# Attention plus gMLP block: the second chunk's modulation issued two pieces behind a product over two blocks instead of four over one, and the last spatial weight sums put behind other products

## The chip, the cores and the metric

The kernel runs on one core of a Trainium2 chip. The metric is device time in microseconds (us), median of several executions. PE is TensorE, PEld its weight loads, DVE is VectorE, ACT is ScalarE.

## The reference, cut to what matters

```python
def _B_ref(x, w_in, w_sp, b_sp, w_out):      # S = 2048, D = 1024, Fh = 1792
    z = _gelu(jnp.einsum('bsd,df->bsf', x, w_in))
    z1 = z[..., :Fh].copy()
    z2 = _layernorm(z[..., Fh:], axis=-1)
    g = jnp.einsum('ts,bsf->btf', w_sp, z2) + b_sp[None, :, None]
    return jnp.einsum('bsf,fd->bsd', z1 * g, w_out)
# ... attention comes first (32 heads), then:
h = _layernorm(x, axis=-1) * (1 + cb) + sb   # the "modulation" of this study
x = x + gb * _B_ref(h, B_w_in, B_w_sp, B_b_sp, B_w_out)
```

Attention fills the time up to about 1130 us, its output projection the time up to 1320 us. The change touches the products of `h` with `w_in` (1310 to 1490 us), and the preparation of `w_sp` for the spatial product that follows.

## The kernel before

Each matrix product is done in blocks of two by two. Seven sub-products take the place of eight, at the price of sums of operands (on VectorE, ahead of TensorE) and of results (ScalarE copies a PSUM bank out, a "snap"; VectorE adds another bank to it). A `Block` has seven products, numbered 1 to 7; bank "a" serves 1, 6, 5 and 3 in turn, so TensorE can't start product 6 before ScalarE has copied what 1 left. `hooks` are functions queued right after a given product; this is where all side work is placed.

```python
BANK = {1: "a", 6: "a", 5: "a", 3: "a", 2: "c", 7: "b", 4: "b"}
def finish(self, n):
    ps = self.ps[self.BANK[n]]
    if n == 1:   self.s = self.snap(ps, 1)                      # ScalarE copy
    elif n == 2: self.out(1, 1, ps, self.s)                     # VectorE sum, gelu two products later
    elif n == 6: self.x = self.snap(ps, 2)
    elif n == 5: self.out(2, 2, self.ps["b"], self.snap(ps, 3))
    elif n == 3: self.out(1, 2, ps, None)
    elif n == 4: self.out(2, 1, ps, self.x)
    for fn in self.hooks.get(n, ()):
        fn()
    # ... functions put off by after(n, fn) run here when their count is down
```

Two streams of blocks are interleaved product by product (`dual`). Each stream runs product 1 of a block, then 3 and 4 of its previous block, then 2, 6, 7, 5. The second chunk (rows 1024 to 2047) is modulated in place once its transposed load has landed, sixteen pieces of 128x512 in four quarters:

```python
def mod_h(c, i, j):
    t = hT[c, i, j]
    for dc in range(4):
        k = 8 + 4 * j + dc
        if c == 0:
            nc.scalar.activation(t[:, dc, :], t[:, dc, :], ACT.Identity,
                                 scale=cols_l[:, 8 + k:9 + k], bias=cols_l[:, k:k + 1])
        else:
            nc.vector.tensor_scalar(out=t[:, dc, :], in0=t[:, dc, :], scalar1=cols_l[:, 8 + k:9 + k],
                                    scalar2=cols_l[:, k:k + 1], op0=ALU.mult, op1=ALU.add)
# ...
for n, m in enumerate((3, 1, 2, 4)):
    # ... loads of the quarters
    z2b[3].on((1, 2, 6, 7)[n], lambda q=HQ[(n + 2) % 4]: mod_h(1, *q))   # four pieces at once
    z1b[2].on((1, 2, 6, 7)[n], lambda m=n + 1: h_sum(1, m))              # needs the modulated quarters
```

Near the end of the stage, the hooks of z1 block n make the four small weight sums of z1 block n+1 (`w1_sum`, after products 2, 6, 7 and 5). Behind them, at the same four hooks, one task each is taken from a list; the last eight tasks are the last sums over `w_sp` (128x1024):

```python
b.on((2, 6, 7, 5)[k - 1], lambda m=m, k=k: w1_sum(*seq[m], k))
# ...
z2b[15].on(4, ..., lambda: tasks.extend(sums[8:]), ...)
for b in z2b[9:] + z1b[7:]:
    for m in (2, 6, 7, 5):
        b.on(m, work())
```

In the profiles these are: L1217 the modulation on VectorE, L1214 the modulation on ScalarE, L1388 a small weight sum, L1440 a spatial sum, L1043 the sum of a bank and a snap, L1038 a snap, L1320 a gelu, L1465 a piece of layer norm on VectorE, L995 every product of these blocks.

The softmax here doesn't subtract the row's maximum and nothing guards it: scores larger than these inputs give would overflow.

Of the kernel before, what the change touches and what calls it, by code (L numbers as in the profile page):

```python
# [16 lines left out]
def kernel(  # L17
# [1111 lines left out]
    for n in range(2, 6):  # L1129
        for k, m in enumerate((6, 7, 7, 5)):  # L1130
            q = 4 * (n - 2) + k
# [69 lines left out]
    def load_h(c, i, j):  # L1201

        t = hT[c, i, j] = heap.take("hT", [P, 4, 512], FP16)
        t0 = c * 1024 + i * 512
        nc.sync.dma_start(out=t[:], in_=h2_dram[t0:t0 + 512, j * 512:(j + 1) * 512],
                          transpose=True)

    def mod_h(c, i, j):

        t = hT[c, i, j]  # L1210
        for dc in range(4):
            k = 8 + 4 * j + dc
            if c == 0:
                nc.scalar.activation(t[:, dc, :], t[:, dc, :], ACT.Identity,  # L1214
                                     scale=cols_l[:, 8 + k:9 + k], bias=cols_l[:, k:k + 1])
            else:
                nc.vector.tensor_scalar(out=t[:, dc, :], in0=t[:, dc, :],  # L1217
                                        scalar1=cols_l[:, 8 + k:9 + k],
                                        scalar2=cols_l[:, k:k + 1], op0=ALU.mult, op1=ALU.add)

    def h_sum(c, n):

        s = hs.setdefault(c, {})
        s[n] = hT[c, 1, 0] if n == 3 else heap.take(f"hs{n}", [P, 4, 512], FP16)
        a, b = {1: (hT[c, 1, 0], hT[c, 1, 1]), 2: (s.get(1), hT[c, 0, 0]),
                3: (hT[c, 0, 0], hT[c, 1, 0]), 4: (hT[c, 0, 1], s.get(2))}[n]
        fn = nc.vector.tensor_add if n == 1 else nc.vector.tensor_sub
        fn(out=s[n][:], in0=a[:], in1=b[:])
# [15 lines left out]
    def w2_sum(k, n):  # L1244

        t = w2t.setdefault(k, {})
        t[n] = w2[k, 0, 1] if n == 1 else heap.take(f"w2_t{n}", [P, 4, FC], FP16)
        a, b = {1: (bf(w2[k, 0, 1][:]), bf(w2[k, 0, 0][:])), 2: (bf(w2[k, 1, 1][:]), t.get(1)),
                3: (bf(w2[k, 1, 1][:]), bf(w2[k, 0, 1][:])),
                4: (bf(w2[k, 1, 0][:]), t.get(2))}[n]  # L1250
        nc.vector.tensor_sub(out=t[n][:], in0=a[:], in1=b[:])
# [34 lines left out]
    HQ = ((1, 0), (1, 1), (0, 0), (0, 1))  # L1286
    for n, q in enumerate(HQ):
        (wos[5] if n < 3 else wos[6]).on((6, 7, 5, 1)[n], lambda q=q: load_h(0, *q))
        wos[6].on((2, 6, 7, 5)[n], lambda q=q: mod_h(0, *q))
# [47 lines left out]
    def z2_block(c, k, m):  # L1337
        def operands(n):
            h = h_op(c, n)
            b = {1: (0, 0), 2: (1, 0), 3: (1, 1)}.get(n)  # L1340
            w = bf(w2[(k,) + b][:]) if b else w2t[k][{4: 4, 5: 1, 6: 2, 7: 3}[n]][:]
            return ([h[:, dc, m * P:(m + 1) * P] for dc in range(4)],
                    [w[:, dc, :] for dc in range(4)])

        def out(i, j, ps, snap):
            ti = 8 * c + 4 * (i - 1) + m
            f0 = (j - 1) * 2 * FC + k * FC
            z = short("z2")[:, 0:FC]
            gelu(z, ps, snap)

            def stats():
                nc.vector.bn_stats(out=z_st[:, ti, 2 * (j - 1) + k, :], in_=z)
                nc.sync.dma_start(z2_dram[ti, :, f0:f0 + FC], z)
                left_[ti] -= 1
                if not left_[ti]:
                    nc.vector.bn_aggr(out=z_mv[:, ti, :], in_=z_st[:, ti])
            after(4, stats)

        b = Block(operands, copy_snap, out, FC)
        b.on(4, lambda: done_with_h(c))  # L1360
        return b
# [28 lines left out]
    def z1_block(c, p):  # L1390
        def operands(n):
            h = h_op(c, n)
            b = {1: (0, 0), 2: (1, 0), 3: (1, 1)}.get(n)
            if b:
                w = [w1[c, p][:, 4 * b[0] + dc, b[1] * P:(b[1] + 1) * P] for dc in range(4)]
            else:
                w = [w1t[c, p][:, {4: 3, 5: 0, 6: 1, 7: 2}[n], dc, :] for dc in range(4)]
            return w, [h[:, dc, :] for dc in range(4)]

        def out(i, j, ps, snap):  # L1400
            if (c, p) not in z1T:
                z1T[c, p] = heap.take("z1T", [P, 2, 1024], FP16)
            gelu(z1T[c, p][:, j - 1, (i - 1) * 512:i * 512], ps, snap)

        b = Block(operands, copy_snap, out)
        b.on(4, lambda: done_with_h(c))
        return b
# [7 lines left out]
    def load_w(c, k, j):  # L1415

        t0 = c * 1024 + j * 512
        for u in range(2):
            t = W[k, j, u] = heap.take(f"w{k}{j}", [P, 4, 512], FP16)
            nc.sync.dma_start(out=bf(t[:]), in_=B_w_sp[t0:t0 + 512, (2 * k + u) * 512:  # L1420
                                                       (2 * k + u + 1) * 512], transpose=True)
# [67 lines left out]
    def work(n=1):  # L1489
        def go():  # L1490
            for _ in range(n):
                if tasks:
                    tasks.pop(0)()
        return go

    seq = [(c, p) for c in range(2) for p in range(NG)]
    z2b = [z2_block(c, k, m) for k in range(2) for c in range(2) for m in range(4)]
    z1b = [z1_block(*s) for s in seq]
# [5 lines left out]
    for n, s in enumerate(seq):  # L1504
        b = z1b[n]
# [8 lines left out]
    z2b[2].on(7, lambda: load_w2(1))  # L1514
    for n, m in enumerate((3, 1, 2, 4)):
        (wos[7] if n < 2 else z2b[0]).on((3, 4, 7, 5)[n], lambda q=HQ[(n + 2) % 4]: load_h(1, *q))
        z2b[3].on((1, 2, 6, 7)[n], lambda q=HQ[(n + 2) % 4]: mod_h(1, *q))
        z1b[2].on((1, 2, 6, 7)[n], lambda m=n + 1: h_sum(1, m))
        z2b[4 + n // 2].on((7, 5)[n % 2], lambda m=m: w2_sum(1, m))
        z2b[6 + n].on(2, lambda n=n: load_w(0, *WQ[n]))  # L1520
# [3 lines left out]
        z2_norms(), [load_z(0, p, k) for p in range(2) for k in range(2)])))  # L1524
    z2b[9].on(1, lambda: tasks.extend(scale_w() + sums[:8]))
    for b in z2b[9:] + z1b[7:]:
        for m in (2, 6, 7, 5):
            b.on(m, work())
    z1b[9].on(4, lambda: load_b(0))
    norms = []  # L1530
# [326 lines left out]
```

## Time and profile before

| | before |
|---|---|
| median of the first 3 runs | 1757.61 us (1756.5 to 1757.78) |
| span of the profiled run (its time: 1754.26 us) | 1752.4 us |
| PE busy | 1734.1 us, 99% |

The page's first lines and the first line of its chain of waits:

```profile
span 1752.4 us, 23647 instructions
...
PE 1734.1 (99%) x8414; PEld 795.6 (45%) x8414; DVE 1522.7 (87%) x2324; ACT 1297.7 (74%) x1530; POOL 31.3 (2%) x39
...
PE 93%; DVE 4%; DMA 1%; ACT 1%; issue 1%; SPq 0%; DVEq 0%; ACTq 0%
```

TensorE is the bound, so only a moment in which it stands still can be won. Busy time is the wrong place to look for those (a matmul's record outlasts the distance to the next one: 379 ns against 216 ns), so the useful reading is the distance between starts. Four matmuls of 512 columns that are not held up take 0.86 us, four of 448 columns 0.76 us. The timeline of TensorE (start, duration, engine, line, operation, out<-in, count, idle before it) then shows the stops around the modulation:

```profile
1351.48 1.03 PE L995 MATMUL a<-hT,w_13040 128*128 128x512 f16 x4
1352.71 0.92 PE L995 MATMUL b<-s_slots,h_slots 128*128 128x448 f16 x4 [0.20 <-DVE sum L1043]
1354.29 1.02 PE L995 MATMUL a<-tx,h_slots 128*128 128x512 f16 x4 [0.66 <-ACT snap L1038]
```

From 1351.48 to 1352.71 is 1.23 us where 0.86 would do, a gap of 0.37; from 1352.71 to 1354.29 is 1.58 where 0.76 would do, a gap of 0.83. The bracket alone understates both, since it counts from a modelled end. What kept the sum and the snap is in the timelines of VectorE and ScalarE:

```profile
1349.57 1.36 DVE L1217 TENSOR_SCALAR hT<-hT,cols_l 128x512 f16<-128x512 f16 x4
...
1352.04 0.61 DVE L1043 TENSOR_TENSOR sum<-b,snap 128x448 f32<-128x448 f32 x1
```

```profile
1352.69 0.58 ACT L1320 ACTIVATE z_13178<-sum 128x448 f16<-128x448 f32 x1 [2.67 <-DVE sum L1043]
1353.17 1.07 ACT L1038 ACTIVATE snap<-a 128x512 f32<-128x512 f32 x2
```

VectorE has no idle time from 1348 to 1355 (in the table of windows below, 7.00 of 7), and the lump of four at 1349.57 belongs to a product that ended near 1346.6, so it is some 3 us behind. The sum of bank "b" runs at 1352.04, and TensorE waits for that bank. A gelu on ScalarE waits 2.67 us for the same sum, and the snap that frees bank "a" stands behind the gelu. So one late sum stops TensorE twice. A third gap of 0.29 us follows at 1363.1.

The second place is at 1471 to 1475 us, first TensorE, then VectorE:

```profile
1470.80 1.03 PE L995 MATMUL b<-hT,w_t 128*128 128x512 f16 x4
1471.80 1.04 PE L995 MATMUL a<-hs_13248,s_slots 128*128 128x512 f16 x4
1472.68 1.03 PE L995 MATMUL a<-hs_13196,w_t 128*128 128x512 f16 x4
1474.27 1.04 PE L995 MATMUL b<-hT,s_slots 128*128 128x512 f16 x4 [0.57 <-DVE s_slots L1388]
```

```profile
1471.66 0.68 DVE L1440 TENSOR_TENSOR h_slots<-w_13586,h_slots 128x1024 f16<-128x1024 f16 x1
...
1473.19 0.68 DVE L1440 TENSOR_TENSOR w_t_14467<-w_13588,w_13499 128x1024 f16<-128x1024 f16 x1
1473.79 0.42 DVE L1388 TENSOR_TENSOR s_slots<-h_slots 128x512 f16<-128x512 bf16 x1
```

The weight sum that TensorE wants at 1473.5 is only begun at 1473.79, behind two spatial sums (L1440) that nobody wants before 1490. The gaps are 0.14 and 0.73 us.

The busy times of this table of windows are quoted later (columns: stretch, its length, then busy time and instructions per engine):

```profile
1334.00:1348.00 14.00, 14.00 (x72) 6.85 (x71) 12.52 (x30) 8.75 (x17) 0.00 (x0) 1.00 1.00 296
1348.00:1355.00 7.00, 6.13 (x30) 2.74 (x29) 7.00 (x17) 3.53 (x7) 0.00 (x0) 1.00 0.33 100
```

### The profile page before, as it was taken

The numbers are of one execution on the slowest core, as the hardware profiler recorded it, in microseconds if no ns is written. First come the engines' busy times: TensorE is split into PE (matmuls) and PEld (weight loads), VectorE is DVE, ScalarE is ACT, GpSimd is POOL, SyncE is SP. The second block draws the span as 40 slices with busy tenths as digits, with TensorE's granted clock in tenths as the row PEclk, the third lists the DMA queues.
The fourth block names the chain that finished last, engine by engine and source line by source line (L and its number), as shares of the span: only waits on it lengthen the run. The fifth ranks groups of instructions, "written<-read, shape, count | busy, mean of one in ns | idle before, by whom it ended". The sixth has DMA issues, their size and how long they took to land.

```text
span 1752.4 us, 23647 instructions
## 1 busy us (share of the span) xinstructions
PE 1734.1 (99%) x8414; PEld 795.6 (45%) x8414; DVE 1522.7 (87%) x2324; ACT 1297.7 (74%) x1530; POOL 31.3 (2%) x39
## 2 busy tenths in 40 slices
PE   7999999999999999999999999999999999999999
PEld 4444444444444444444444444444444444444444
DVE  6898898898988899998999988898889788778975
ACT  6998889999999999999999999711235666737500
POOL 1000000000000000000000000000000000000000
PEclk9999999999999999999999999999999999999999
DMA  8575456645434643544643464758858544548222
GB/s 253 132 183 142 115 142 160 163 121 133 122 95 137 171 104 96 151 141 131 163 120 103 119 186 130 195 138 210 209 159 217 146 120 122 180 120 229 60 78 97
DMA packets 465896, 253.79 MB, mean 145 GB/s; under 512 B 310640, under 2 KB 425584, under 8 KB 465776
## 3 DMA queue, kind: packets, MB, share of 16 engines
q1 hardware_dynamic: 465776, 252.26, 53.9%
q8 instruction: 66, 1.08, 0.3%
q14 instruction: 54, 0.44, 0.1%
HBM read 142.08 MB, written 55.59 MB: 113 GB/s over the span
## 4 chain that ended last, share of the span: by engine, by line
PE 93%; DVE 4%; DMA 1%; ACT 1%; issue 1%; SPq 0%; DVEq 0%; ACTq 0%
PE sps L510 24%; PE ops L787 24%; PE a L995 17%; PE b L995 9%; PE c L995 4%; PE qa L491 4%; PE qps L408 4%; PE qb L491 3%; PE bo L1619 1%; ACT pt L850 1%; DMA wm<-in_w_mod_dram 1%; PE a_11083 L995 1%; DVE sum L1043 0%; DVE stats L155 0%; PE a L1717 0%
## 5 line engine op out<-in xcount | busy, mean ns | idle before, releaser
L850 ACT ACTIVATE pt<-sps 128x1024 bf16<-128x1024 f32 x1008 | 1003.7, 1023 | 77.7 <-PE sps L510 34.8
L510 PE MATMUL sps<-qT,kT 128*128 128x512 bf16 x2048 | 609.2, 379 | 2.3 <-ACT pt L850 1.2
L787 PE MATMUL ops<-pt,v_sb 128*128 128x512 bf16 x2048 | 598.9, 379 | 0.0
L510 PEld LDWEIGHTS <-kT 128*128 128x128 bf16 x2048 | 199.6, 98 | 247.2 <-issue 14.5
L787 PEld LDWEIGHTS <-v_sb 128*128 128x128 bf16 x2048 | 200.1, 98 | 243.2 <-issue 1.6
L1038 ACT ACTIVATE snap<-a 128x512 f32<-128x512 f32 (+1 forms) x111 | 60.5, 564 | 99.2 <-PE a L995 82.8
L995 PEld LDWEIGHTS <-h_slots 128*128 128x128 f16 (+1 forms) x756 | 73.9, 98 | 87.5 <-issue 1.4
L866 DVE COPY ou<-ops 128x512 f32<-128x512 f32 x126 | 81.1, 685 | 31.5 <-PE ops L787 28.8
L408 PE MATMUL qps<-h1T,wq_t 128*128 128x512 bf16 x288 | 96.7, 379 | 0.0
L1468 ACT ACTIVATE zr<-zr,z_nm,z_rs 128x256 f16<-128x256 f16 x96 | 47.9, 586 | 48.2 <-DMA zr<-z_dram 48.2
L1043 DVE TENSOR_TENSOR sum<-b,snap 128x512 f32<-128x512 f32 (+1 forms) x76 | 50.0, 659 | 36.0 <-ACT snap L1038 18.7
L666 DVE TENSOR_TENSOR oT<-ou,rbc 128x1024 bf16<-128x1024 f32 x62 | 75.3, 1215 | 1.1 <-DMA rbc<-rec_dram 1.1
L476 DVE COPY tx<-qa 128x512 f32<-128x512 f32 x66 | 45.4, 688 | 30.6 <-PE qa L491 30.6
L644 DVE TENSOR_REDUCE den<-pT 128x8 f32<-128x1024 bf16 x58 | 68.6, 1183 | 0.0
L491 PE MATMUL qa<-h1s,wq_t 128*128 128x512 f16 x176 | 63.1, 379 | 0.0
L995 PEld LDWEIGHTS <-wq_t 128*128 128x128 f16 (+1 forms) x390 | 38.1, 98 | 45.1 <-issue 0.3
L995 PEld LDWEIGHTS <-s_slots 128*128 128x128 f16 (+1 forms) x363 | 35.4, 98 | 43.3 <-DVE s_slots L1388 1.5
L491 PEld LDWEIGHTS <-wq_t 128*128 128x128 bf16 (+1 forms) x352 | 34.4, 98 | 41.5
L149 POOL TENSOR_TENSOR rstd<-var,neg_half 128x1 f32<-128x1 f32 x30 | 25.9, 862 | 1295.7 <-DVE var L147 1228.4
L471 DVE TENSOR_TENSOR qT<-qb,tx 128x512 bf16<-128x512 f32 x66 | 45.2, 684 | 0.7
L408 PEld LDWEIGHTS <-wq_t 128*128 128x128 bf16 x288 | 28.2, 98 | 33.9 <-issue 0.6
L491 PEld LDWEIGHTS <-tx 128*128 128x128 f16 x264 | 25.8, 98 | 31.2
(979 smaller groups left out, 2576.9 us busy)
## 6 DMA issues: line engine op xcount, KB each, us to landing
rbc<-rec_dram SPq DMA_DIRECT2D x63, 512.0 KB
v_sb<-in_A_v_cache_dram SPq DMA_DIRECT2D x40, 512.0 KB
oT_dram<-oT SPq DMA_DIRECT2D x62, 256.0 KB
sums_dram<-pacc SPq DMA_DIRECT2D x58, 256.0 KB
wm<-in_w_mod_dram SPq DMA_DIRECT2D x8, 1024.0 KB
wq_t<-in_A_wq_dram SPq DMA_DIRECT2D x7, 1024.0 KB
zr<-z_dram SPq DMA_DIRECT2D x12, 512.0 KB
oq<-oT_dram SPq DMA_DIRECT2D x11, 512.0 KB
```

The lines of the kernel that those rows point to most:

```text
L408: nc.tensor.matmul(box["ps"][:], weights[:, dc, hc:hc + DH], src[:, dc, q0:q0 + 512], start=(n == 0), stop=(n == KD - 1))
L491: nc.tensor.matmul(box["b" if m in (2, 7, 4) else "a"][:], *operand(m, dc), start=(m in (1, 2, 7) and dc == 0), stop=(dc == 3), skip_group ...
L510: nc.tensor.matmul(sps[:, j * 512:(j + 1) * 512], kts[h][:, kb * P:(kb + 1) * P], qts[(h, qh)][:, j * 512:(j + 1) * 512], start=True, stop ...
L644: nc.vector.tensor_reduce(out=den[:], in_=state[i]["pT"][:], op=ALU.add, axis=mybir.AxisListType.X)
L666: nc.vector.tensor_mul(out=oT, in0=state[i]["ou"][:], in1=state[i]["rbc"][:])
L787: nc.tensor.matmul(o_ps[j][:], vs[halves[i][0]][:, kb, :], pt_tiles[g][:, j * 512:(j + 1) * 512], start=(kb == 0), stop=(kb == NKB - 1))
L850: nc.scalar.activation(pt_tiles[g], s_tiles.pop(g)[:], ACT.Exp, scale=SCALE, **bias)
L866: nc.vector.tensor_copy(out=ou[:, j * 512:(j + 1) * 512], in_=o_ps[j][:])
L995: nc.tensor.matmul(self.ps[self.BANK[n]], a, b, start=(n in (1, 2, 7) and k == 0), stop=(k == len(lhs) - 1), skip_group_check=True)
L1038: nc.scalar.activation(t, ps, ACT.Copy)
L1043: nc.vector.tensor_add(out=t, in0=ps, in1=snap)
L1468: nc.scalar.activation(z, z, ACT.Identity, scale=z_rs[:, q:q + 1], bias=z_nm[:, q:q + 1])
```

## The change

The intent, by the title that the change came with, is to spread the modulation thinly, two pieces behind a product instead of four, over the third and fourth z2 blocks instead of the fourth alone, one piece on ScalarE and one on VectorE; and to move the last spatial sums away from the hooks where the weight sums are due. The whole diff:

```diff
-    def mod_h(c, i, j):
+    def mod_h(c, i, j, dcs=range(4), by_act=True):
 
         t = hT[c, i, j]
-        for dc in range(4):
+        for dc in dcs:
             k = 8 + 4 * j + dc
-            if c == 0:
+            if by_act:
                 nc.scalar.activation(t[:, dc, :], t[:, dc, :], ACT.Identity,
                                      scale=cols_l[:, 8 + k:9 + k], bias=cols_l[:, k:k + 1])
             else:
@@
-        z2b[3].on((1, 2, 6, 7)[n], lambda q=HQ[(n + 2) % 4]: mod_h(1, *q))
+        for k in range(2):
+            z2b[2 + n // 2].on(((2, 6), (7, 5), (1, 2), (6, 7))[n][k], *[
+                lambda q=HQ[(n + 2) % 4], dc=2 * k + a: mod_h(1, *q, (dc,), not a)
+                for a in range(2)])
@@
     for b in z2b[9:] + z1b[7:]:
-        for m in (2, 6, 7, 5):
+        for m in (2, 6, 7, 5) if b not in z1b[10:] else (1, 3, 7):
             b.on(m, work())
```

## The prediction

> **What bounds the kernel.** TensorE. The engine table gives PE 1734.1 us busy of 1752.4 (99%), at full clock; the chain of waits is 93% PE. The Trainium skill ("Perfetto Trace Analysis", Identifying the Most-Contended Engine) warns that matmul busy time is a poor measure because matmuls are pipelined, so I took distances between matmul starts: 216 ns for 512 columns, 189 ns for 448, back to back almost everywhere. The excess over that is 11.2 us in the first 40 us, 8.0 us through attention, and only 3.1 us between 1300 and 1500 us, which the diff touches. No matmul is added or removed, so the reachable gain lies inside those 3 us.
>
> **Part A: modulation.** Before, sixteen VectorE pieces (128x512 f16; the timeline shows 1.37 us for four) run in lumps at 1339.7, 1344.1, 1345.9 and 1349.6 us. VectorE is 12.5 us busy of 14 in 1334 to 1348 and 7.0 of 7 in 1348 to 1355 (table of windows), and 3 us behind: the last lump belongs to a product that ends near 1346.6. A gelu on ScalarE then waits 2.7 us for a late VectorE sum, the PSUM copy behind it is late, and TensorE stops: 0.37 us at 1352.7 (for a sum), 0.83 at 1354.3 and 0.29 at 1363.1 (for copies). Gaps of 0.32 and 0.44 us at 1327 and 1330.5 lie ahead of this and stay.
>
> After, eight pieces stay on VectorE (0.34 us each; 2.7 us removed) and eight go to ScalarE (2.92 us for four in the first chunk's modulation, 0.73 each, 5.8 us added), one of each per hook, from about 1334.6 to 1347 us. The transposed loads landed at 1324.1, 1328.8, 1334.7 and 1336.7 us, before each quarter's first use, so nothing waits for a load. VectorE's backlog at 1352 should go, and with it 1.2 to 1.5 us of gaps. Against that, ScalarE's 8.75 us busy in 1334 to 1348 become 14.6 of 14: slightly overfull. TensorE needs a copy two to five products (0.76 to 0.87 us each) later; I allow 0 to 0.6 us of new gaps at 1340 to 1349.
>
> **Part B: last spatial sums.** Eight VectorE sums (128x1024, 0.6 us each) run at 1469.3 to 1479.8 us among the small weight sums of the next z1 block, due two products later. TensorE loses 0.14 us at 1471.8 and 0.73 at 1474.3 to those weight sums. After, the eight sit behind products 1, 3 and 7 (on 7 the weight sum precedes them), spread over 1472 to 1488. This recovers 0.5 to 0.87 us. VectorE has little idle in 1476 to 1492 (15.25 of 16 busy), so norm pieces and first gate sums may come 0.6 us later against some 3 us of slack: cost 0 to 0.3 us.
>
> **Sum.** A gains 1.3 less 0.3, B 0.7 less 0.1: about 1.6 us, from 1757.6 to 1756.0 us (0.1%); 8 times in 10 between 1754.4 and 1757.7. Chances: faster by over 2% 0.005, within 2% 0.99, slower by over 2% 0.005.
>
> **What would show it.** No TensorE gap at 1352 to 1355, nor at 1471 to 1475; the last modulation ends before 1348 instead of 1351; ScalarE full near 1334 to 1348; VectorE 2.7 us less busy; span near 1750.8.
>
> **What would make it wrong.** ScalarE's overfull stretch delays copies and stops TensorE near 1340 to 1350 by as much as at 1354; or the later sums hold up norms or gate sums, opening a gap at 1485 to 1496; or the gap at 1354 came from the weight sums beside the modulation and stays.

## The result, and the profile after

Ratios in this document are the mean time of one kernel's runs over that of the other's of the same rounds, so not quite the ratio of the medians quoted.

| | before | after |
|---|---|---|
| median | 1757.05 us (4 runs, 1754.78 to 1757.78) | 1753.49 us (4 runs, 1753.12 to 1754.07) |
| ratio | | 0.9982, 95% interval 0.9965 to 0.9999 |
| span of the profiled run | 1752.4 us | 1752.3 us |

The median lies below the forecast's range, and the two profiled spans are equal although the medians differ by 3.6 us. Both need an explanation. The first lines of the page of after:

```profile
span 1752.3 us, 23530 instructions
...
PE 1728.6 (99%) x8299; PEld 795.6 (45%) x8414; DVE 1522.5 (87%) x2324; ACT 1298.5 (74%) x1530; POOL 30.7 (2%) x39
```

PE's busy time fell by 5.5 us for no good reason: 115 of 8414 matmul records are missing from this trace. All 8414 weight loads are there, in the same order in both, so from here on the traces are laid side by side by weight load. The table gives how much later (positive) or earlier (negative) a given load starts than in the profiled run of before, in us:

| weight load no. (its start in before) | 300 (33 us) | 6300 (1304 us) | 7000 (1447 us) | 7170 (1483 us) | last (1749 us) |
|---|---|---|---|---|---|
| after | +1.09 | +2.19 | +0.71 | -0.18 | +0.10 |

The code up to load 6300 is the same. The changed kernel's profiled run lost 1.09 us in its first 33 us and 1.10 more in attention, before any of the change was reached; it then won 1.48 us at the modulation and 0.89 us at the spatial sums, and gave back 0.28 us, a net 2.09 us. The equal spans are an accident of the start and of attention.

TensorE's timeline where before stopped at 1352.71 and 1354.29:

```profile
1353.66 1.03 PE L995 MATMUL a<-hT,w_13044 128*128 128x512 f16 x4
1354.53 0.92 PE L995 MATMUL b<-s_slots,h_slots 128*128 128x448 f16 x4
1355.28 1.03 PE L995 MATMUL a<-tx,h_slots 128*128 128x512 f16 x4
```

The starts are 0.87 and 0.75 us apart: no gap. VectorE (and ScalarE below) at the same place:

```profile
1350.62 0.72 DVE L1217 TENSOR_SCALAR hT<-hT,cols_l 128x512 f16<-128x512 f16 x2
...
1352.45 0.61 DVE L1043 TENSOR_TENSOR sum<-b,snap 128x448 f32<-128x448 f32 x1
```

```profile
1353.10 0.58 ACT L1320 ACTIVATE z_13178<-sum 128x448 f16<-128x448 f32 x1 [2.02 <-DVE sum L1043]
1353.58 1.07 ACT L1038 ACTIVATE snap<-a 128x512 f32<-128x512 f32 x2
```

This run is 2.18 us late at this point, so the sum at 1352.45 stands at 1350.27 on the clock of before, where it stood at 1352.04: 1.77 us earlier. The snap came forward by the same 1.77 us (1353.58 less 2.18 against 1353.17). VectorE is not less busy; it did the same work sooner, as the windows moved by the same 2 us show:

```profile
1336.00:1350.00 14.00, 14.00 (x72) 6.86 (x71) 14.00 (x35) 9.13 (x18) 0.00 (x0) 1.00 1.01 296
1350.00:1357.00 7.00, 7.00 (x35) 3.27 (x34) 7.00 (x16) 4.56 (x10) 0.00 (x0) 1.00 0.44 127
```

VectorE was idle 1.48 us of the first window before, and is idle no time after. ScalarE has 9.13 us in it, not the 14.6 that the prediction added up: no ScalarE piece was made. The instructions of the ScalarE line confirm it (count, durations in ns, first and last start); the last one starts at 1293 us, and these are the first chunk's:

```profile
L1214 ACT ACTIVATE h_slots<-h_slots,cols_l x8: 801/803/805, 1272.0 to 1282.6; 128x512 f16<-128x512 f16 x8
L1214 ACT ACTIVATE hT<-hT,cols_l x8: 798/801/804, 1284.8 to 1293.0; 128x512 f16<-128x512 f16 x8
```

The second place is clean too (timelines of TensorE and VectorE of after), with the wanted weight sum now begun at 1472.70 (1.8 us earlier, after taking off the 0.71 us by which this run is late):

```profile
1472.37 1.03 PE L995 MATMUL a<-hs_13248,s_slots 128*128 128x512 f16 x4
1473.23 1.03 PE L995 MATMUL a<-hs_13196,w_t 128*128 128x512 f16 x4
1474.10 1.03 PE L995 MATMUL b<-hT,s_slots 128*128 128x512 f16 x4
```

```profile
1472.70 0.42 DVE L1388 TENSOR_TENSOR s_slots<-h_slots 128x512 f16<-128x512 bf16 x1
1473.03 0.69 DVE L1440 TENSOR_TENSOR h_slots<-w_13586,h_slots 128x1024 f16<-128x1024 f16 x1
```

A small stop is new, at 1484 to 1487 us (TensorE's timeline of after). From 1485.36 to 1486.45 is 1.09 us where 0.86 would do:

```profile
1485.36 1.03 PE L995 MATMUL a<-hs_13196,w_t 128*128 128x512 f16 x4
1486.45 1.04 PE L995 MATMUL b<-hT,w_t 128*128 128x512 f16 x4
```

TensorE waits there for weight sums again (L1388, at 1484.02 and 1485.98), which now stand behind moved spatial sums and pieces of the layer norm.

### The profile page after: what moved, and what is told of

Same layout as the page of the kernel before. It is cut to its first block, busy times and chain, and to the rows that moved or that the text cites. A ratio compares the mean times of both kernels' runs of the same rounds, so it can differ in the third digit from the quotient of the medians. Undisturbed runs are those within 1.5% of the kernel's fastest.

```text
span 1752.3 us, 23530 instructions
## 1 busy us (share of the span) xinstructions
PE 1728.6 (99%) x8299; PEld 795.6 (45%) x8414; DVE 1522.5 (87%) x2324; ACT 1298.5 (74%) x1530; POOL 30.7 (2%) x39
## 4 chain that ended last, share of the span: by engine, by line
PE 90%; DVE 5%; DMA 2%; issue 1%; ACT 1%; SPq 0%; DVEq 0%; ACTq 0%
PE ops L787 23%; PE sps L510 22%; PE a L995 17%; PE b L995 9%; PE c L995 5%; PE qa L491 4%; PE qps L408 3%; PE qb L491 3%; PE bo L1622 1%; ACT pt L850 1%; DMA wm<-in_w_mod_dram 1%; PE a_11083 L995 1%; DVE sums_3250 L872 0%; DVE den L644 0%; DVE ou L866 0%
## 5 line engine op out<-in xcount | busy, mean ns | idle before, releaser
L510 PE MATMUL sps<-qT,kT 128*128 128x512 bf16 x1986 | 596.4, 379 | 4.0 <-ACT pt L850 2.1
L995 PEld LDWEIGHTS <-h_slots 128*128 128x128 f16 (+1 forms) x700 | 68.5, 98 | 79.7 <-DVE h_slots L1065 0.3
```

The costliest lines, as they stand in the source:

```text
L510: nc.tensor.matmul(sps[:, j * 512:(j + 1) * 512], kts[h][:, kb * P:(kb + 1) * P], qts[(h, qh)][:, j * 512:(j + 1) * 512], start=True, stop ...
L995: nc.tensor.matmul(self.ps[self.BANK[n]], a, b, start=(n in (1, 2, 7) and k == 0), stop=(k == len(lhs) - 1), skip_group_check=True)
```

## The experiments

Theory 1: closing TensorE's gaps is all that the change does, worth about 2 us; the rest of the 3.6 us is the runs' own spread. Theory 2: the change really saves about 3.5 us. Theory 3: chance. Within the modulation part there are three rival reasons: the earlier start, the smaller lumps, or less load on VectorE.

All kernels gave correct results. Times with 95% intervals of the ratio to before are in this table, and the aligned gains after it.

| run | median us (runs) | before, same chip | ratio (95%) |
|---|---|---|---|
| e1_both | 1753.79 (5) | 1755.23 (9) | 0.9992 (0.9979 to 1.0004) |
| e2_null | 1755.33 (5) | 1755.23 (9) | 1.0003 (0.9990 to 1.0015) |
| e3_a_only | 1753.25 (5) | 1755.23 (9) | 0.9993 (0.9981 to 1.0006) |
| e4_b_only | 1755.10 (5) | 1755.23 (9) | 0.9999 (0.9985 to 1.0012) |
| e5_true_split | 1753.47 (5) | 1754.70 (9) | 0.9990 (0.9977 to 1.0004) |
| e6_lumps_early | 1753.11 (4) | 1754.70 (9) | 0.9989 (0.9975 to 1.0002) |
| e7_split_late | 1755.24 (4) | 1754.70 (9) | 0.9999 (0.9986 to 1.0013) |
| e8_norm_on_act | 1753.04 (5) | 1754.70 (9) | 0.9985 (0.9973 to 0.9998) |
| e9_gelu_later | 1752.40 (4) | 1754.72 (7) | 0.9989 (0.9972 to 1.0005) |

The first four share their nine runs of before, the next four share nine others. Gains in the aligned traces against the profiled run of before, in us (negative is faster):

| run | shift at load 300 | shift at load 6300 | load 6300 to 7000 (modulation) | load 7000 to the end (sums) | both |
|---|---|---|---|---|---|
| after | +1.09 | +2.19 | -1.48 | -0.61 | -2.09 |
| e1_both | +0.33 | +1.65 | -1.48 | -0.61 | -2.08 |
| e2_null | -0.50 | +0.32 | +0.01 | +0.01 | +0.01 |
| e3_a_only | -0.59 | -0.06 | -1.48 | +0.01 | -1.47 |
| e4_b_only | +1.02 | +1.76 | +0.01 | -0.60 | -0.59 |
| e5_true_split | -0.90 | -0.06 | -1.43 | -0.61 | -2.04 |
| e6_lumps_early | -0.34 | +0.00 | -1.44 | +0.00 | -1.44 |
| e7_split_late | +0.84 | +1.62 | -0.14 | +0.00 | -0.14 |
| e8_norm_on_act | +1.28 | +2.14 | -1.47 | -0.89 | -2.36 |
| e9_gelu_later | -1.57 | -1.54 | -1.96 | -0.89 | -2.85 |

### e1_both: the changed kernel again

No edit.

> The changed kernel once more, beside before on the same chip. Theory 1 (closed TensorE gaps are all of it): aligned by weight loads, the lead over before between 1350 and 1500 us is 2.0 us (0.2 us either way), and the times differ by 2 us (1.2 to 2.8); the rest of the 3.6 us between the medians so far is start-up and run-to-run difference. Theory 2 (the change really saves about 3.5 us, some of it outside the edited stage): times differ by 3 us or more, with a gain in the aligned trace outside 1310 to 1500 us. Theory 3 (chance): the times differ by less than 0.7 us.

The aligned lead is 2.08 us, equal to the first trace's 2.09. The mean over five runs is 1.7 us below the mean of before's nine (1753.16 and 1754.88), inside theory 1's range and well short of theory 2's 3 us. The interval of the ratio includes 1, so from these times alone chance would not be excluded; the traces exclude it.

### e2_null: before, as a kernel

No edit.

> Before, word for word, submitted as a kernel. Theory 1 expects no difference of the means beyond 0.8 us, but single runs that spread over 2 to 3.5 us, and in the aligned trace shifts of 1 us or more that arise in the first 40 us and in attention, from the clock's half-speed stretches at the start. Theory 2 expects a narrow spread, under 1.5 us.

The means differ by 0.2 us, and single runs spread over 2.3 us (the nine of before over 3.6). The gaps at 1353, 1354, 1363, 1472 and 1474 us are the same as in the first trace of before to 4 ns, and from load 6300 to the end the two traces agree within 0.01 us. So the edited stage is repeatable to a hundredth of a microsecond, while the start is not: over the ten traces of the table the same code reaches load 6300 between 1.54 us earlier and 2.19 us later than in the first trace, and at load 300 it is already between 1.57 us earlier and 1.28 us later. Theory 2 has fallen.

### e3_a_only: the modulation alone

The changed kernel with the hooks of the sums as in before:

```diff
-        for m in (2, 6, 7, 5) if b not in z1b[10:] else (1, 3, 7):
+        for m in (2, 6, 7, 5):
```

> Only the modulation's new places (all pieces still run on VectorE, as the trace of the changed kernel shows). Theory 1: the gaps near 1353, 1354 and 1363 us close, a lead of 1.4 us in the aligned trace, time 1.4 us less than before (0.6 to 2.2); the two gaps near 1472 and 1474 stay. Rival (the reach of the modulation's lumps is not the cause; VectorE is as full as before and the gaps stay without part B): lead under 0.5 us.

The three gaps near 1353 to 1363 close, worth 1.48 us, and the two near 1472 and 1474 stay at 0.14 and 0.73 us. The times (mean 1.4 us lower) fit but don't settle it.

### e4_b_only: the sums alone

Before with only that one line of the diff.

> Only the new places of the last spatial sums. Theory 1: gaps of 0.14 and 0.73 us near 1472 and 1474 close, and a new one of about 0.4 us opens near 1485 from weight sums behind the moved sums: lead 0.6 us net in the aligned trace (1.05 gained, 0.45 given back), time 0.6 us less. Rival (the give-back near 1485 comes from part A): lead 1.0 us, no gap near 1485.

The two gaps close (0.89 us, where I had read 1.05 by looking at a weight load that itself waited), and the stop near 1485 opens, 0.28 us: net 0.60. It comes with the sums' new places and not with the modulation. (The mean time is 0.3 us lower, which settles nothing.) The two parts add up: 1.48 + 0.60 against 2.08 for both.

### e5_true_split: the split made real

The changed kernel with `a` bound too:

```diff
-                lambda q=HQ[(n + 2) % 4], dc=2 * k + a: mod_h(1, *q, (dc,), not a)
+                lambda q=HQ[(n + 2) % 4], dc=2 * k + a, a=a: mod_h(1, *q, (dc,), not a)
```

> The changed kernel with the split that its title names really made: the engine of each piece is bound when the hook is made, so that eight pieces run on ScalarE and eight on VectorE. The prediction's theory (ScalarE overfull): eight ScalarE pieces of about 0.73 us appear, VectorE is 2.7 us less busy, and TensorE gets new gaps of up to 0.6 us between 1336 and 1352; the time is then no better than the changed kernel's. Rival (there is room on both): no new gap, aligned trace within 0.1 us of the changed kernel from 1310 us to the end, so the split is worth nothing because the gaps were closed already.

Now there are eight more ScalarE pieces, 24 where there were 16 (lines as above: count, durations, first and last start), and VectorE is 2.1 us less busy in all than in before (1520.6 against 1522.7). The table of windows follows:

```profile
L1214 ACT ACTIVATE hT<-hT,cols_l x12: 801/804/834, 1282.5 to 1347.5; 128x512 f16<-128x512 f16 x12
L1214 ACT ACTIVATE h_slots<-h_slots,cols_l x10: 801/802/803, 1269.8 to 1337.6; 128x512 f16<-128x512 f16 x10
L1214 ACT ACTIVATE wq_t<-wq_t,cols_l x2: 807/807/807, 1338.7 to 1341.7; 128x512 f16<-128x512 f16 x2
```

```profile
1334.00:1348.00 14.00, 14.00 (x72) 6.81 (x70) 12.33 (x28) 13.39 (x25) 0.00 (x0) 1.00 0.98 291
```

The duration of one, 0.80 us, agrees with the Trainium skill ("ScalarE: Activation LUTs", What ACT_TABLE_LOAD costs): its 280 ns plus 0.833 ns an element for one pointer operand and 93 ns for a second give an estimate of 799 ns at 512 elements. ScalarE is 13.4 us busy of 14 and still costs TensorE only one new gap of 0.05 us, at 1342 us. The aligned gain is 1.43 us, against 1.48 without the split. The prediction's worry about a full ScalarE was wrong in size, and the split that the title names is worth nothing here: the gaps were closed without it.

### e6_lumps_early: whole lumps at the new start

Before (with the new arguments of `mod_h`) with each lump of four at the hook where the change starts that quarter:

```diff
-        z2b[3].on((1, 2, 6, 7)[n], lambda q=HQ[(n + 2) % 4]: mod_h(1, *q))
+        z2b[2 + n // 2].on((2, 7, 1, 6)[n],
+                           lambda q=HQ[(n + 2) % 4]: mod_h(1, *q, range(4), False))
```

> Before, with the lumps of four VectorE pieces kept whole but each put at the hook at which the change starts that quarter (products 2 and 7 of the third z2 block, 1 and 6 of the fourth); sums as before. If the earlier start is what counts (VectorE work moved out of the full stretch into its idle times near 1338 to 1344): the gaps near 1353, 1354 and 1363 close, aligned gain of 1.3 to 1.5 us as for the modulation part alone. If the size of the lumps counts (1.37 us ahead of a due sum): gaps of 0.5 us or more stay or appear between 1338 and 1364.

The gaps close all the same: 1.44 of the 1.48 us, with one new gap of 0.03 us at 1343. The last lump, from VectorE's timeline, is still whole, but starts at 1345.60 where it started at 1349.57; this run is level with before at load 6300, so the times can be compared as they stand:

```profile
1345.60 1.37 DVE L1217 TENSOR_SCALAR hT<-hT,cols_l 128x512 f16<-128x512 f16 x4
```

TensorE's timeline where before stopped; the starts are 0.86 and 0.76 us apart:

```profile
1351.51 1.03 PE L995 MATMUL a<-hT,w 128*128 128x512 f16 x4
1352.37 0.92 PE L995 MATMUL b<-s_slots,h_slots 128*128 128x448 f16 x4
1353.13 1.03 PE L995 MATMUL a<-tx,h_slots 128*128 128x512 f16 x4
```

Cutting the lumps in two is worth 0.04 us; starting them earlier is worth the rest. The Trainium skill ("Perfetto Trace Analysis", Optimizing Scalar/DVE Operations) advises "breaking up instructions" where an unsaturated engine causes bubbles elsewhere. No run here tests that: no instruction was broken up, only groups of four were parted, on an engine without idle time, and the place in time decided.

### e7_split_late: half the load, old places

Before (with the new arguments of `mod_h`), same four hooks, but two of each four pieces on ScalarE:

```diff
-        z2b[3].on((1, 2, 6, 7)[n], lambda q=HQ[(n + 2) % 4]: mod_h(1, *q))
+        z2b[3].on((1, 2, 6, 7)[n], lambda q=HQ[(n + 2) % 4]: (
+            mod_h(1, *q, (0, 2), True), mod_h(1, *q, (1, 3), False)))
```

> Before, with the four lumps at their old hooks, but two pieces of each four on ScalarE and two on VectorE; sums as before. If VectorE's backlog is the cause of the gaps near 1353 to 1363, taking 2.7 us of work from it closes them just as the earlier start does: aligned gain 1.2 to 1.5 us. If only the place in time counts, or ScalarE's added 5.8 us delay its copies as much: gain under 0.7 us.

The gain is 0.14 us. VectorE did become freer, but the delay moved to ScalarE, where pairs of 1.51 us, at 1346.07, 1348.37 and 1350.25, now stand between the copies. The last of them and what follows, from ScalarE's timeline:

```profile
1350.25 1.51 ACT L1214 ACTIVATE hT<-hT,cols_l 128x512 f16<-128x512 f16 x2
1351.66 0.62 ACT L1320 ACTIVATE z1T<-sum 128x512 f16<-128x512 f32 x1
1352.18 1.01 ACT L1038 ACTIVATE snap<-a 128x512 f32<-128x512 f32 x2
```

TensorE stops at 1352.81 for that copy, as its timeline shows. From 1350.66 is 2.15 us where 0.86 would do, a gap of 1.29 us, nearly as much as the three gaps of before together:

```profile
1350.66 1.03 PE L995 MATMUL a<-hT,h_slots 128*128 128x512 f16 x4
1352.81 1.02 PE L995 MATMUL a<-hs,w_t 128*128 128x512 f16 x4 [1.13 <-ACT snap L1038]
```

Of the five arrangements, the three that start early (VectorE in pairs, VectorE in fours, both engines one by one) gain 1.43 to 1.48 us, and the two that start late gain 0 and 0.14. The earlier start is the cause. What less load on VectorE alone would do at the old places, with nothing added to ScalarE, was not tried.

### e8_norm_on_act: against the 0.28 us given back

The changed kernel with one more pair of the layer-norm pieces on ScalarE:

```diff
-            norms.extend([lambda k=k, t=t: norm_z(0, *k, (t, t + 1), t != 4)
+            norms.extend([lambda k=k, t=t: norm_z(0, *k, (t, t + 1), t != 4 and (k, t) != ((0, 1), 2))
```

> The changed kernel with one more pair of the layer-norm pieces (128x256, rows 2 and 3 of the second half's first operand) on ScalarE, to take 0.6 us from VectorE just ahead of the two late weight sums near 1484 and 1486. If those 0.28 us are VectorE's backlog from the moved sums and the norm pieces together: both gaps close and nothing opens, aligned lead over before of 2.3 to 2.4 us instead of 2.1; the time cannot show 0.3 us. Rival (ScalarE, 12.8 of 16 us busy there, then holds up copies): a new gap of 0.1 us or more between 1480 and 1496.

The late weight sums come 0.5 us sooner and the stop is gone in TensorE's timeline (from 1483.55 to 1484.41 is 0.86 us, and the two products from there to 1486.14 take 1.73):

```profile
1483.55 1.03 PE L995 MATMUL b<-hT,w_t 128*128 128x512 f16 x4
1484.41 1.89 PE L995 MATMUL a<-hs,w_t 128*128 128x512 f16 x8
1486.14 1.03 PE L995 MATMUL b<-hT,w_t 128*128 128x512 f16 x4
```

The aligned gain is 2.36 us. So the 0.28 us were VectorE's backlog of moved sums and norm pieces together, and nothing opened elsewhere.

### e9_gelu_later: the gaps that no kernel had touched

On top of e8, the gelu of the first two z2 blocks is queued three products later instead of two:

```diff
-    def gelu(dst, ps, snap):
+    def gelu(dst, ps, snap, lag=2):
@@
-            after(2, lambda: nc.scalar.activation(dst, t, ACT.Gelu_apprx_tanh))
+            after(lag, lambda: nc.scalar.activation(dst, t, ACT.Gelu_apprx_tanh))
@@
-            gelu(z, ps, snap)
+            gelu(z, ps, snap, 3 if (c, k) == (0, 0) and m < 2 else 2)
```

> The kernel of the last run (changed kernel, one more norm pair on ScalarE) with the gelu of the first two z2 blocks queued one product later, so that two PSUM copies no longer stand behind a gelu that waits 2.5 us for a VectorE sum. If the two gaps near 1327 and 1330.5 (0.32 and 0.44 us, there in every kernel so far) are made by this order on ScalarE: 0.4 to 0.76 us of them close, aligned lead over before of 2.8 to 3.1 us. Rival (the copies are late for another reason, or the next VectorE sum then comes late): lead stays near 2.4 us or falls.

The gap near 1327 us (0.32) is gone and the one near 1330 shrank from 0.44 to 0.27: 0.49 us more, an aligned lead of 2.85 us, and the lowest median of all (1752.40 us). This beats both kernels in the trace; in time the interval of its ratio, with four runs, still includes 1. What holds the last 0.27 us was not tried.

## Why the prediction was right or wrong

**Level and range: wrong, and this is the step that failed.** The prediction says "about 1.6 us, from 1757.6 to 1756.0 us" and put the lower end at 1754.4; the median is 1753.49. The term that was mis-sized is the starting level. I took the median of three runs (1756.5 to 1757.78), though the profile that I read all gaps from belonged to a run of 1754.26 us, below all three. The 30 later runs of before whose clocks are listed have a mean of 1754.97 us (1753.16 to 1756.98). Against that mean the level was 2.6 us too high. The gain was 0.5 us too small (the modulation was put at 1.0 us net and measured 1.48, the sums at 0.6 and measured 0.61): 1754.97 less 2.08 is 1752.9, where e1 measured a mean of 1753.16 and the first four runs 1753.54. A range drawn from three runs was too narrow for runs that spread over 3.8 us. Two of those three runs even lie above all 30 later ones, so the later spread doesn't cover them: why before was slower in the first measurement (median 1757.05, against 1754.70 to 1755.23 beside the experiments) stays open.

**Where that spread comes from: partly shown.** The profile's clock records have stretches of 3.41 us at half speed in the first 35 us, two of them in the profiled run of after (16.3 and 29.9 us), one in that of before (17.2 us), none in some others. The 12 runs of before with a mean clock of 0.998 average 1756.06 us, the 18 with 0.999 or 1.0 average 1754.25; all four runs of the first measurement of after were at 0.998. The Trainium skill ("TensorE: Matmul & The Clock Gate", What's actually happening) describes a free-running window of 3413 ns, so that the warm-up differs from run to run; the length agrees with these records. e4's trace lists no half-speed stretch and was yet 1.02 us late at load 300, but its first clock record is only at 22.44 us. The matmuls of line 193 (128x512, durations in ns) tell what came before, first e4, then e2, whose clock is recorded from 15.0 us:

```profile
L193 PE MATMUL zps<-zeros x8: 511/634/634, 10.7 to 22.2; 128*128 128x512 bf16 x8
L193 PE MATMUL zps<-zeros x8: 376/505/631, 10.9 to 20.8; 128*128 128x512 bf16 x8
```

A record of 634 ns is that of the recorded half-speed stretches, one of 379 ns that of full speed. In e4 none of the eight was at full speed up to 22.2 us, and two of them start 0.43 us apart (17.67 and 18.10 us) instead of 0.216; so TensorE was slow there too, and the mean clock of 1.0 listed for that run does not count it. The shift at load 300 goes with this in all eleven traces: the four at full clock without a break from 13.2 to 15.1 us on (e2, e5, e6, e9) are 0.34 to 1.57 us early, the three with one stretch that ends near 20 to 21 us (before, e1, e3) lie between 0.59 early and 0.33 late, the two whose records begin at 22.4 us (e4, e7) are 0.84 and 1.02 late, and the two with a stretch at 29.9 us (after, e8) 1.09 and 1.28 late. No run set the clock, so this is a pattern and not a test. The spread within these groups, and the 0 to 1.3 us that arise in attention, stay open.

**Modulation: the gain was right, the mechanism half right.** "VectorE's backlog at 1352 should go, and with it 1.2 to 1.5 us of gaps" measured 1.48. But "eight go to ScalarE" was false: the lambda binds its engine late and all pieces stay on VectorE. So "ScalarE full near 1334 to 1348" (9.1 us of 14) and "VectorE 2.7 us less busy" (1522.5 against 1522.7) both failed. The backlog shrank (by 1.77 us at the sum that held up TensorE) because the same work began earlier, in VectorE's 1.48 idle us of that window, not because it grew less: e6 shows the first, e7 that half the load moved to ScalarE at the old places gains 0.14 us. That "the last modulation ends before 1348 instead of 1351" failed too: it ended at 1351.33 in the run of after, 1349.15 on the clock of before. The allowance of 0.3 us for an overfull ScalarE was for something that didn't happen, and where it was made to happen (e5) it cost 0.05.

**Sums: right.** 0.5 to 0.87 us forecast, 0.89 measured, just above it; 0 to 0.3 us of cost forecast, 0.28 measured. The cost fell at 1484 to 1487 us on weight sums, not on "norms or gate sums" at 1485 to 1496.

**Within 2%: right.** The change is worth 2.1 us, 0.12% of the time. **Span near 1750.8: wrong**, 1752.3, since that run was 2.19 us late before the change was reached.

## What to carry to other kernels

Where one engine is the bound, count its gaps between starts, and treat their sum as the ceiling of any reordering. Here, side work on a full engine was best moved forward into the idle time before the full stretch (1.43 to 1.48 us); moving half of it to another engine at the same moment mostly moved the wait (0.14 us). Align two traces by an instruction that is complete in both before believing a difference of spans, and take the level to forecast from more runs than three.

## What the Trainium skill lacked or had wrong

- "TensorE: Matmul & The Clock Gate", Back-to-back issue gap: it gives about 131 ns for a sustained stream of load and matmul pairs at N=512. These runs sustain 216 ns at 512 columns (four in 0.86 us) and 189 ns at 448, which is the page's formula for an isolated matmul.
- "TensorE: Matmul & The Clock Gate", What's actually happening: it calls the ramp less than 1% of a typical span and advises against fitting a specific count of slow matmuls. It is small here too, but runs of the same kernel at a mean clock of 0.998 and of 0.999 or more differ by 1.8 us on average, nearly the whole effect under study.
- "Perfetto Trace Analysis": I found nothing there of matmul records missing from a trace. Here 115 of 8414 were missing in five of eleven traces, and PE's busy time fell by 5.5 us with them, while the weight loads were complete in all.
